# Loading, centring and multiplying the first two row tiles in another order

## The chip, the cores and the metric

The kernel runs on one core of a Trainium2 chip. The core has five engines that run side by side: TensorE (PE in the profile; its weight loads are PEld), VectorE (DVE), ScalarE (ACT), GpSimdE (POOL) and SyncE (SP). They wait for each other through semaphores. SyncE and ScalarE each issue loads and stores on a queue of their own. The metric is the device time of one execution in microseconds (us), and of several runs the median counts.

## The reference

Both halves of the model get the same normalised input. Only this matters here:

```
xn = (x - mean(x)) / sqrt(var(x) + 1e-5)          # x: 2048 x 512, bf16
q, k, v = xn @ wqkv                               # 32 heads of 16
phi(a) = [softmax(a @ w_phi), softmax(-a @ w_phi)]
o = phi(q) @ (phi(k)^T v) / (phi(q) @ sum(phi(k)) + 1e-6)
h = (xn @ w_gate) * (xn @ w_up)                   # 2048 x 1792
out = x + o @ wo + h @ w_down
```

## The kernel before, in words

The 2048 rows of x are 16 tiles of 128 rows. TensorE contracts over the partitions, so that every product with xn needs xn transposed: `xnT`, four blocks q of 128 columns for each tile. Tiles 4 to 15 are normalised on VectorE and transposed by DMA. Tiles 0 to 3, with which the kernel starts, take a shorter way: they are only centred, transposed on TensorE, and their scale (`rstd`) is applied later, on what is computed from them.

The way of a first tile t:

- `load_x_half` (L276) or `load_x` (L271) brings it in; a half is 256 of the 512 columns. A load that is issued earlier on a queue is begun earlier there.
- `ln_mean_split(t)` (L435) takes the mean in two parts at once: ScalarE sums the second half of the columns (an ACTIVATE and a read of its accumulator, L228), VectorE the first half (L438). For tiles 0 and 1 VectorE's part waits for the first half alone.
- `ln_center_split(t)` (L442) subtracts both parts in two instructions of 256 columns on VectorE (L445); `ln_center_whole(t)` (L449) does it in one of 512.
- `x_transpose(t, b, h, eng)` (L477) transposes half h, that is two blocks, on TensorE (L485) into PSUM bank b; then ScalarE (L228), or VectorE if it is named (L494), copies the result into `xnT`.
- `v_matmul(t, b, qs)` (L540) multiplies the blocks of `xnT` by the blocks of the v weights (`load_v`, L313), four matmuls of 512 columns for a tile, accumulated in bank b. All matmuls of this kind have line 247, in the helper `mm`.

Each call of `load_x_half`, `load_x` or `load_v` is one load on its queue. Before the change the queues begin so, in order: SyncE tile 0's first half, tile 1's first half, tile 2, v blocks 0 and 2, tile 3, then the gate and up weights (`load_gu`); ScalarE tile 0's second half, tile 1's second half, v blocks 1 and 3.

`warm` (L1008) issues matmuls on constants whose result nobody reads, into bank 7. The kernel begins with seven of 512 columns, and an eighth that waits for tile 0.

A small scheduler stands behind all this. Each helper records steps with what they read and write; `_order` (L1262) then plans the order on every engine by estimated costs. Steps recorded while `sc.pin` is set keep their recorded order on their engine. This is so for all of TensorE's steps, and from L329 to L350 and L1019 to L1056 for the steps of every engine. An instruction thus waits behind whatever is recorded ahead of it on the same engine, even if its own inputs are there. The order of the start is therefore the order of the lines L1017 to L1056: first the means and centrings of tiles 0 and 1, the transposes of both, then the v matmuls of both tiles together, block by block (q = 1 and q = 0 of both, tile 2's transposes, q = 3 and 2 of both). After them come tile 2's v matmuls and `g0a`, the first half of the first unit of the gate product (four matmuls of 256 columns), tile 3's transposes, and `u0a`, the same for the up product.

After the start, TensorE computes the gate and up products (L247) for all tiles with the attention's products in between, and at last the output products.

Of the kernel before, what the change touches and what calls it, by code (L numbers as in the profile page):

```python
# [10 lines left out]
ALU = mybir.AluOpType  # L11
AX = mybir.AxisListType

PE, ACT, DVE, POOL, SP = "PE", "ACT", "DVE", "POOL", "SP"
# [95 lines left out]
def bass_parallel_sum__linear_kernel_hedgehog__glu_gated_bilinear__prompt_kernel(  # L110
    nc: bass.Bass,
    A_x: bass.AP,
    A_wqkv: bass.AP,
    A_w_phi: bass.AP,
    A_wo: bass.AP,
    B_x: bass.AP,
    B_w_gate: bass.AP,
    B_w_up: bass.AP,
    B_w_down: bass.AP,
    out: bass.AP,  # L120
):
    with ExitStack() as es:
        _build(nc, es, A_x, A_wqkv, A_w_phi, A_wo, B_w_gate, B_w_up, B_w_down, out)


def _build(nc, es, A_x, A_wqkv, A_w_phi, A_wo, B_w_gate, B_w_up, B_w_down, out):
# [77 lines left out]
    def sb(name, lo, n):  # L204
        off = layout[name] + lo
        return arena[:, off:off + n]
# [4 lines left out]
    def sbf(name, lo, n):  # L211
        off = layout[name] + 2 * lo
        return arena[:, off:off + 2 * n].bitcast(F32)

    def bank(b, lo=0, n=512):
        return psum[:, b * 512 + lo:b * 512 + lo + n]

    def bank16(b, lo, n):
        return psum16[:, b * 1024 + lo:b * 1024 + lo + n]
# [3 lines left out]
    def act(out_ap, in_ap, reads, writes, func=ACTF.Copy, scale=1.0, bias=None, accum=None):  # L223
        kw = {} if bias is None else {"bias": bias}
        if accum is not None:
            kw["accum_out"] = accum
        n = out_ap.free_size()
        return sc.step(ACT, lambda e: e.activation(out=out_ap, in_=in_ap, func=func, scale=scale, **kw),  # L228
                       reads, writes, 130.0 + 0.833 * n)

    def dve(fn, reads, writes, n, rate=1.04):
        return sc.step(DVE, fn, reads, writes, 140.0 + rate * n)
# [7 lines left out]
    def mm(out_ap, pairs, reads, b, start=True, stop=True, skip=False, also=()):  # L240
        npair = len(pairs)

        def fn(e):
            ins = None
            for i, (l, r) in enumerate(pairs):
                kw = {"skip_group_check": True} if skip else {}
                ins = e.matmul(out_ap, lhsT=l, rhs=r, start=start and i == 0, stop=stop and i == npair - 1, **kw)  # L247
            return ins
        return sc.step(PE, fn, reads, [("ps", b), *also], npair * pe_cost(out_ap.free_size()))
# [8 lines left out]
    def x_tile(t):  # L258
        return sb("x", t * 512, 512)

    def xnT(q, lo, n):
        return sb("xnT", q * S_TOK + lo, n)


    def rows(ap, t0, n):
        g, r = divmod(t0, 4)
        if g == 0:
            return ap[t0 * 128:(t0 + n) * 128, :].rearrange("(r p) d -> p r d", r=n)
        return ap[g * 512:(g + 1) * 512, :].rearrange("(p r) d -> p r d", r=4)[:, r:r + n, :]

    def load_x(t0, n, eng=SP):  # L271
        o = sb("x", t0 * 512, n * 512).rearrange("p (t d) -> p t d", t=n)
        i = rows(x_flat, t0, n)
        sc.dma(eng, lambda e: e.dma_start(o, i), [], [("x", t) for t in range(t0, t0 + n)], n * 131072)

    def load_x_half(t, h, eng):  # L276
        c = slice(h * 256, h * 256 + 256)
        o, i = x_tile(t)[:, c], rows(x_flat, t, 1)[:, 0, c]
        sc.dma(eng, lambda e: e.dma_start(o, i), [], [("x", t) if h else ("x", t, 0)], 65536)  # L279
# [18 lines left out]
    def load_w(eng, o, i, key, nbytes):  # L298
        sc.dma(eng, lambda e: e.dma_start(o, i), [], [key], nbytes)
# [13 lines left out]
    def load_v(eng, q):  # L313
        load_w(eng, wv_v[:, q, :], A_wqkv[q * 128:(q + 1) * 128, 1024:1536], ("wv", q), 131072)
# [12 lines left out]
    pool(c_fn, [], ["const"], 300)  # L327

    sc.pin = True  # L329
    for t in range(2):  # L330
        load_x_half(t, 0, SP)
        load_x_half(t, 1, ACT)
    load_x(2, 1)
    load_v(ACT, 1)
    load_v(SP, 0)
    load_v(ACT, 3)
# [68 lines left out]
    def xn_tile(t):  # L405
        return sb("xn", (t % 4) * 512, 512)

    mu = sbf("mu", 0, ND)
# [24 lines left out]
    mua = sbf("mua", 0, ND)  # L433

    def ln_mean_split(t):  # L435
        act(xn_tile(t)[:, 256:], x_tile(t)[:, 256:], [("x", t)], [("mu", t)], scale=1.0 / 512.0,
            accum=mu[:, t:t + 1])
        dve(lambda e: e.tensor_scalar(out=xn_tile(t)[:, :256], in0=x_tile(t)[:, :256], scalar1=1.0 / 512.0,  # L438
                                      scalar2=0.0, op0=ALU.mult, op1=ALU.add, accum_out=mua[:, t:t + 1]),
            [("x", t, 0) if t < 2 else ("x", t)], [("mua", t)], 256)  # L440

    def ln_center_split(t):  # L442
        for h in range(2):
            hs = slice(h * 256, (h + 1) * 256)
            dve(lambda e, hs=hs: e.tensor_scalar(out=xn_tile(t)[:, hs], in0=x_tile(t)[:, hs], scalar1=mua[:, t:t + 1],  # L445
                                                 scalar2=mu[:, t:t + 1], op0=ALU.subtract, op1=ALU.subtract),
                [("x", t), ("mua", t), ("mu", t)], [("xn", t, h)], 256, 0.27)

    def ln_center_whole(t):  # L449
        dve(lambda e: e.tensor_scalar(out=xn_tile(t), in0=x_tile(t), scalar1=mua[:, t:t + 1],  # L450
                                      scalar2=mu[:, t:t + 1], op0=ALU.subtract, op1=ALU.subtract),
            [("x", t), ("mua", t), ("mu", t)], [("xn", t, 0)], 512, 0.27)
# [24 lines left out]
    def x_transpose(t, b, h, eng=ACT):  # L477
        n = NQ // 2
        qs = slice(h * n, (h + 1) * n)

        def fn(e):
            ins = None
            for i in range(n):
                q = h * n + i
                ins = e.transpose(bank16(b, i * 128, 128), xn_tile(t)[:, q * 128:(q + 1) * 128], ident)  # L485
            return ins
        sc.step(PE, fn, [("xn", t, h if t < 2 else 0), "ident"], [("ps", b)], n * 60.0)
        o = sb("xnT", 0, NQ * S_TOK).rearrange("p (q s) -> p q s", q=NQ)[:, qs, t * 128:(t + 1) * 128]
        i = bank16(b, 0, n * 128).rearrange("p (q s) -> p q s", q=n)
        w = [("xnT", t, h)]  # L490
        if eng == ACT:
            act(o, i, [("ps", b)], w)
        else:
            dve(lambda e: e.tensor_copy(out=o, in_=i), [("ps", b)], w, n * 128)  # L494
# [45 lines left out]
    def v_matmul(t, b, qs=((0, 1), (2, 3)), start=True, stop=True):  # L540
        for n, part in enumerate(qs):
            mm(bank(b), [(xnT(q, t * 128, 128), wv_v[:, q, :]) for q in part],
               ([("xnT", t, part[0] // 2)] if t < ND else [("xnT", t)]) + [("wv", q) for q in part], b,
               start=start and n == 0, stop=stop and n == len(qs) - 1)
# [463 lines left out]
    def warm(n, w=512, after=()):  # L1008
        def fn(e):
            ins = None  # L1010
            for _ in range(n):
                ins = e.matmul(bank(7, 0, w), lhsT=nc.const_aps.tensor(1.0, (128, 128), BF16),
                               rhs=nc.const_aps.tensor(1.0, (128, w), BF16), start=True, stop=True)
            return ins
        sc.step(PE, fn, after, [("ps", 7)], n * w * 0.8)

    warm(7)  # L1017
    warm(1, 512, [("x", 0)])
    sc.pin = True  # L1019
    ln_mean_split(0)  # L1020
    ln_mean_split(1)
    ln_center_split(0)
    ln_center_split(1)
    x_transpose(0, 2, 0)
    ln_mean_split(2)
    x_transpose(0, 3, 1)
    warm(1, 128)
    x_transpose(1, 4, 0, DVE)
    ln_center_whole(2)
    x_transpose(1, 5, 1, DVE)  # L1030
    warm(1, 128)
    for q in (1, 0):
        for t in range(2):
            v_matmul(t, t, ((q,),), start=q == 1, stop=False)
    x_transpose(2, 6, 0)
    x_transpose(2, 4, 1, DVE)
    for t in range(2):
        v_matmul(t, t, ((3,), (2,)), start=False)
    ln_mean_split(3)
    ln_center_whole(3)  # L1040
    (g0a, u0a, g0b, u0b), gate0 = up_unit(*ups.pop(0), pairs, 2)
# [366 lines left out]
```

The softmax here doesn't subtract the row's maximum and nothing guards it: scores larger than these inputs give would overflow.

## Time and profile before

| | us |
|---|---|
| median of 5 runs (lowest, highest) | 214.39 (214.08, 214.93) |
| the profiled execution | 214.34 |
| its span, first to last instruction | 212.6 |
| TensorE busy | 209.0 (98% of the span) |
| VectorE / ScalarE / GpSimdE busy | 165.9 / 144.8 / 108.7 |
| first instruction of TensorE (a warm-up) | 0.82 |
| first v matmul | 5.81 |
| end of the first gate half unit, `g0a` | 9.61 |

The profile covers one execution. The page has the busy time of each engine, the span in 40 slices, the chain of work that ended last, the costliest groups of instructions and the loads. The timeline lists an engine's instructions by start; the chain cut to a window lists what the end waited for, by start, length and what; the view of stretches gives busy times and counts of each engine between two moments. In a line such as `L247 PE MATMUL ps<-arena 128x512`, L247 is the line of the kernel (often a helper's), `ps` is PSUM and `arena` the one SBUF tensor that holds everything. A "q" behind an engine's name (SPq, ACTq) means its queue's issue of a load. The matmuls of TensorE are pipelined: the time shown for one reaches over the start of the next, and so the distance from start to start is what one costs.

### The profile page before, as it was taken

How to read it: one execution, taken by the hardware profiler on the slowest of the kernel's cores; microseconds unless marked ns; L12 is line 12 of the kernel's file. 1: busy time of each engine (PE TensorE's matmuls, PEld its weight loads, DVE VectorE, ACT ScalarE, POOL GpSimd, SP SyncE). 2: the span in 40 equal slices, each digit the busy share in tenths (PEclk: the TensorE clock that was granted, in tenths of full speed). 3: DMA queues.
4: the chain of work that ended last, by engine and by line, in shares of the span. 5: the costliest groups of instructions: out<-in, count | busy, mean ns of one | idle time of the engine just before them, and what ended most of it. 6: DMA issues, size and time to landing. Idle time of an engine off the chain costs nothing.

```text
span 212.6 us, 4050 instructions
## 1 busy us (share of the span) xinstructions
PE 209.0 (98%) x1476; PEld 125.6 (59%) x1476; DVE 165.9 (78%) x281; ACT 144.8 (68%) x350; POOL 108.7 (51%) x137
## 2 busy tenths in 40 slices
PE   8999999999999999999999999999999999999995
PEld 3565444444454444444444444556888898899884
DVE  3588699998986647758889989896888898897622
ACT  5459998885989999987878977564544444432220
POOL 4030393243312448998895472204658549558540
DMA  5999218479400320231321223413255826745411
GB/s 170 284 262 369 107 34 192 83 207 336 90 3 0 49 49 3 57 61 35 72 52 28 49 52 49 102 55 68 45 81 130 192 50 154 173 80 149 123 49 49
DMA packets 49795, 22.29 MB, mean 105 GB/s; under 512 B 38128, under 2 KB 48496, under 8 KB 49776
## 3 DMA queue, kind: packets, MB, share of 16 engines
q1 hardware_dynamic: 49200, 21.65, 42.3%
q10 hardware_dynamic: 576, 0.39, 0.6%
q8 instruction: 11, 0.18, 0.4%
q14 instruction: 8, 0.07, 0.1%
HBM read 11.03 MB, written 2.10 MB: 62 GB/s over the span
## 4 chain that ended last, share of the span: by engine, by line
PE 96%; DMA 2%; DVE 0%; ACTq 0%; ACT 0%; issue 0%
PE ps L247 91%; PE ps L564 2%; PE ps L622 2%; DMA arena<-in_A_wqkv_dram 2%; PE ps L392 1%; DVE arena L935 0%; ACTq L279 0%; PE ps L485 0%; ACT L1206 0%
## 5 line engine op out<-in xcount | busy, mean ns | idle before, releaser
L247 PE MATMUL ps<-arena 128*128 128x512 bf16 (+2 forms) x1160 | 200.1, 330 | 0.2 <-DMA arena<-in_A_wqkv_dram 0.2
L247 PEld LDWEIGHTS ps<-arena 128*128 128x128 bf16 (+1 forms) x1160 | 110.8, 98 | 74.0 <-issue 0.7
L228 ACT ACTIVATE arena<-ps 128x512 bf16<-128x512 f32 (+3 forms) x117 | 59.3, 538 | 17.8 <-PE ps L247 12.4
L228 ACT ACTIVATE arena<-arena 128x32 f32<-128x32 f32 (+8 forms) x131 | 52.4, 424 | 6.0 <-DVE arena L905 3.0
L905 DVE TENSOR_TENSOR arena<-ps,arena 128x512 f16<-128x512 f32 (+1 forms) x56 | 38.4, 686 | 19.6 <-ACT arena L228 13.7
L527 POOL TENSOR_TENSOR arena<-arena 128x1024 bf16<-128x1024 bf16 x16 | 30.9, 1933 | 38.1 <-ACT arena L228 38.1
L228 ACT ACTIVATE arena<-ps,arena 128x512 bf16<-128x512 f32 (+1 forms) x55 | 35.5, 671 | 10.1 <-PE ps L247 10.0
L517 DVE TENSOR_REDUCE arena<-arena 128x64 f32<-128x1024 bf16 x32 | 38.6, 1211 | 3.4 <-ACT arena L228 3.4
L866 POOL TENSOR_TENSOR arena<-arena 128x256 f16<-128x256 f16 x32 | 24.2, 768 | 12.9 <-DMA arena<-arena 11.7
L228 ACT ACTIVATE ps<-ps 128x256 f32<-128x256 f32 x24 | 8.8, 368 | 29.0 <-PE ps L247 29.0
L844 DVE TENSOR_TENSOR arena<-arena 128x896 f16<-128x896 f16 x32 | 23.8, 750 | 3.2 <-PE ps L247 3.1
L935 DVE SCALAR_TENSOR_TENSOR arena<-ps,arena 128x256 bf16<-128x256 f32 (+1 forms) x24 | 13.5, 569 | 10.4 <-PE ps L247 10.0
L784 POOL TENSOR_TENSOR arena<-arena 128x512 f16<-128x512 bf16 x14 | 16.2, 1175 | 4.7 <-DVE arena L905 3.3
L970 POOL TENSOR_TENSOR arena<-arena 128x512 f32<-128x512 f32 x8 | 9.5, 1190 | 17.2 <-ACT arena L228 17.2
L533 POOL TENSOR_TENSOR arena<-arena 128x512 bf16<-128x512 bf16 x16 | 17.1, 1074 | 0.9
L632 DVE TENSOR_TENSOR arena<-ps,arena 128x512 f16<-128x512 f32 x16 | 11.0, 688 | 1.4
L416 DVE BATCH_NORM_STATS2 arena<-arena 128x6 f32<-128x512 bf16 x16 | 10.4, 670 | 0.0
L531 POOL TENSOR_TENSOR arena<-arena 128x32 f32<-128x32 f32 x16 | 4.2, 266 | 9.5 <-ACT arena L228 9.5
L679 DVE BATCH_NORM_STATS2 arena<-arena 128x6 f32<-128x512 bf16 x14 | 9.0, 681 | 0.0
L564 PEld LDWEIGHTS ps<-arena 128*128 128x128 bf16 x128 | 6.1, 97 | 3.5
L813 DVE TENSOR_TENSOR arena<-arena 128x1792 f16<-128x1792 f16 (+1 forms) x8 | 7.0, 903 | 0.0
L622 PEld LDWEIGHTS ps<-arena 128*128 128x128 bf16 x128 | 6.2, 97 | 1.2
(54 smaller groups left out, 68.1 us busy)
## 6 DMA issues: line engine op xcount, KB each, us to landing
arena<-in_A_x_dram SPq DMA_DIRECT2D x8, 256.0 KB, 3.0
out_dram<-arena SPq DMA_DIRECT2D x15, 128.0 KB, 2.0
arena<-in_B_w_down_dram SPq DMA_DIRECT2D x1, 1792.0 KB, 7.5
arena<-in_A_x_dram SPq DMA_DIRECT2D x3, 512.0 KB, 4.2
arena<-arena SPq DMA_TRANSPOSE x44, 3.1
arena<-in_B_w_gate_dram SPq DMA_DIRECT2D x1, 640.0 KB, 8.7
arena<-in_B_w_up_dram SPq DMA_DIRECT2D x1, 640.0 KB, 9.9
arena<-in_B_w_gate_dram SPq DMA_DIRECT2D x1, 512.0 KB, 5.3
```

The costliest lines, as they stand in the source:

```text
L228: return sc.step(ACT, lambda e: e.activation(out=out_ap, in_=in_ap, func=func, scale=scale, **kw), reads, writes, 130.0 + 0.833 * n)
L247: ins = e.matmul(out_ap, lhsT=l, rhs=r, start=start and i == 0, stop=stop and i == npair - 1, **kw)
L517: dve(lambda e: e.tensor_reduce(out=sm, in_=e_v, axis=AX.X, op=ALU.add), [(name, s, 0), (name, s, 1)], [("sums", sr)], 1024)
L527: pool(lambda e: e.tensor_tensor(out=e_w, in0=e_w, in1=r_w, op=ALU.mult), [(name, s, 0), (name, s, 1), ("rs", n)], [(name, s, 0), (name, s ...
L533: pool(lambda e: e.tensor_tensor(out=e_v[:, :, 1, :], in0=e_v[:, :, 1, :], in1=rat[:, :, None].to_broadcast([128, H, 16]), op=ALU.mult), [ ...
L622: ins = e.matmul(bank(b0 + c // 4, (c % 4) * CW, CW), lhsT=ph[:, c, :], rhs=kvz_v[:, c, :], start=True, stop=True)
L632: dve(lambda e: e.tensor_tensor(out=o_tile(t).rearrange("p (b h f) -> p b h f", b=2, f=16), in0=nd[:, :, :, 0:16], in1=w_v[:, r].unsqueeze ...
L784: pool(lambda e, ft=ft: e.tensor_tensor(out=hH_v[:, ft, 0:512], in0=hT_v[:, ft, 0:512], in1=r2w, op=ALU.mult), [("hT", ft, 0), "r2w", ("x" ...
L844: dve(lambda e, k=k, i0=i0, i1=i1, op=op: e.tensor_tensor(out=s_block(p, k), in0=i0, in1=i1, op=op), ks + more, [s_key(p, k)] + over.get(k ...
L866: pool(lambda e, k=k, i0=i0, i1=i1, op=op: e.tensor_tensor(out=so_block(p, k), in0=i0, in1=i1, op=op), ks + [("so", p, m) for m in more], ...
L905: dve(lambda e: e.tensor_tensor(out=h_v[:, ft, sg * 512:(sg + 1) * 512], in0=bank(bu), in1=g, op=ALU.mult), [("ps", bu), ("g", s)] + ([("j ...
L935: dve(lambda e: e.scalar_tensor_tensor(out=o, in0=src, scalar=inv, in1=resid, op0=ALU.mult, op1=ALU.add), keys + [rkey, "inv"], [("ostg", ...
```

## The change

Only tile 0 is still loaded in halves. Tile 1 is loaded whole, by ScalarE's queue, in the slot where its second half was; SyncE's queue loses the other half, so that tile 2 and all that follows there move up by one issue. VectorE's part of tile 1's mean then waits for the whole tile.

`ln_center_split` becomes `ln_center_half`, one half for each call, and the recorded order changes: tile 0's first half is centred ahead of tile 1's mean, its second half after it. Tile 2 is centred before tile 0's second half is transposed. On TensorE tile 0's transposes come first; then tile 0's v matmuls run with tile 1's transposes between them, ahead of all of tile 1's v matmuls; tile 2's transposes stand behind the first v matmul of tile 1. The first copy of tile 1's transposed blocks goes to ScalarE in place of VectorE. The eighth 512-column warm-up and one of the two of 128 columns are gone. What is computed stays the same.

```diff
--- before.py
+++ after.py
@@ -327,10 +327,10 @@
     pool(c_fn, [], ["const"], 300)
 
     sc.pin = True
-    for t in range(2):
-        load_x_half(t, 0, SP)
-        load_x_half(t, 1, ACT)
+    load_x_half(0, 0, SP)
+    load_x_half(0, 1, ACT)
     load_x(2, 1)
+    load_x(1, 1, ACT)
     load_v(ACT, 1)
     load_v(SP, 0)
     load_v(ACT, 3)
@@ -437,14 +437,13 @@
             accum=mu[:, t:t + 1])
         dve(lambda e: e.tensor_scalar(out=xn_tile(t)[:, :256], in0=x_tile(t)[:, :256], scalar1=1.0 / 512.0,
                                       scalar2=0.0, op0=ALU.mult, op1=ALU.add, accum_out=mua[:, t:t + 1]),
-            [("x", t, 0) if t < 2 else ("x", t)], [("mua", t)], 256)
-
-    def ln_center_split(t):
-        for h in range(2):
-            hs = slice(h * 256, (h + 1) * 256)
-            dve(lambda e, hs=hs: e.tensor_scalar(out=xn_tile(t)[:, hs], in0=x_tile(t)[:, hs], scalar1=mua[:, t:t + 1],
-                                                 scalar2=mu[:, t:t + 1], op0=ALU.subtract, op1=ALU.subtract),
-                [("x", t), ("mua", t), ("mu", t)], [("xn", t, h)], 256, 0.27)
+            [("x", t, 0) if t == 0 else ("x", t)], [("mua", t)], 256)
+
+    def ln_center_half(t, h):
+        hs = slice(h * 256, (h + 1) * 256)
+        dve(lambda e: e.tensor_scalar(out=xn_tile(t)[:, hs], in0=x_tile(t)[:, hs], scalar1=mua[:, t:t + 1],
+                                      scalar2=mu[:, t:t + 1], op0=ALU.subtract, op1=ALU.subtract),
+            [("x", t), ("mua", t), ("mu", t)], [("xn", t, h)], 256, 0.27)
 
     def ln_center_whole(t):
         dve(lambda e: e.tensor_scalar(out=xn_tile(t), in0=x_tile(t), scalar1=mua[:, t:t + 1],
@@ -1015,27 +1014,27 @@
         sc.step(PE, fn, after, [("ps", 7)], n * w * 0.8)
 
     warm(7)
-    warm(1, 512, [("x", 0)])
     sc.pin = True
     ln_mean_split(0)
+    ln_center_half(0, 0)
     ln_mean_split(1)
-    ln_center_split(0)
-    ln_center_split(1)
+    ln_center_half(0, 1)
+    ln_center_half(1, 0)
+    ln_center_half(1, 1)
     x_transpose(0, 2, 0)
     ln_mean_split(2)
+    ln_center_whole(2)
     x_transpose(0, 3, 1)
     warm(1, 128)
-    x_transpose(1, 4, 0, DVE)
-    ln_center_whole(2)
+    v_matmul(0, 0, ((1,),), stop=False)
+    x_transpose(1, 4, 0)
+    v_matmul(0, 0, ((0,),), start=False, stop=False)
     x_transpose(1, 5, 1, DVE)
-    warm(1, 128)
-    for q in (1, 0):
-        for t in range(2):
-            v_matmul(t, t, ((q,),), start=q == 1, stop=False)
+    v_matmul(0, 0, ((3,), (2,)), start=False)
+    v_matmul(1, 1, ((1,),), stop=False)
     x_transpose(2, 6, 0)
     x_transpose(2, 4, 1, DVE)
-    for t in range(2):
-        v_matmul(t, t, ((3,), (2,)), start=False)
+    v_matmul(1, 1, ((0,), (3,), (2,)), start=False)
     ln_mean_split(3)
     ln_center_whole(3)
     (g0a, u0a, g0b, u0b), gate0 = up_unit(*ups.pop(0), pairs, 2)
```

## Prediction

> **What bounds the kernel now.** I read the page first, the chain of waits that ended last second, cut to its first 12 us, then the timelines of VectorE (DVE) and the stretches of the start.
>
> ```profile
> PE 96%; DMA 2%; DVE 0%; ACTq 0%; ACT 0%; issue 0%
> ```
>
> ```profile
> 1.71 3.96 DMA arena<-in_A_wqkv_dram
> 5.67 0.14 issue
> 5.81 1.42 PE ps L247 x4
> 7.22 0.22 PE ps L485 x4
> 7.45 2.16 PE ps L247 x12
> 9.61 0.22 PE ps L485 x4
> ```
>
> The columns of the chain are start, length, what. TensorE (PE) sets the end, and from 5.81 on it hands over from group to group without a hole; the records of the single matmuls show no start-to-start distance that is longer than the work from 6.64 us to the end. So whatever TensorE loses or gains before about 6.6 us arrives whole at the end, and the change lives in just that stretch. What the chain waits for ahead of 5.81 is the load of block 1 of the v weights, issued by ScalarE (ACT) as its third load at 1.71 and landed at 5.67.
>
> The second limit is TensorE's own pace. Here are the stretches (length, then the busy time and the number of instructions of each engine):
>
> ```profile
> 0.82:3.76 2.94, 2.94 (x8) 1.01 (x8) 0.64 (x3) 1.97 (x5) 2.23 (x13) 1.00 0.54 142
> ...
> 5.81:6.61 0.80, 0.80 (x2) 0.22 (x3) 0.80 (x5) 0.48 (x3) 0.00 (x0) 1.00 0.89 262
> 6.61:9.01 2.40, 2.40 (x15) 1.22 (x14) 1.17 (x5) 0.78 (x3) 0.00 (x0) 1.00 0.95 277
> ```
>
> The eighth warm-up starts at 3.76, so seven start-to-start steps take 2.94 us, 0.42 each. The first two v matmuls, of the same 128x512 shape, still take 0.40 each (0.80 for x2). The chain's 2.16 us for x12 is eight of 512 columns and four of 256: 0.216 and 0.109 each. The pace doubles at about 6.64 us, 5.82 us after the first warm-up, although the profile prints a granted clock of 1.00 throughout. Two matmuls behind the gate run slow: 2 x (0.40 - 0.216) = 0.37 us of the end.
>
> The third thing to see is how loads land. The lines give queue, count, size and the median time from issue to landing:
>
> ```profile
> arena<-in_A_x_dram SPq DMA_DIRECT2D x2, 128.0 KB, 3.8
> arena<-in_A_wqkv_dram ACTq DMA_DIRECT2D x2, 128.0 KB, 4.0
> ...
> arena<-in_A_x_dram SPq DMA_DIRECT2D x2, 64.0 KB, 2.1
> arena<-in_A_x_dram ACTq DMA_DIRECT2D x2, 64.0 KB, 2.3
> ```
>
> By issue plus landing: tile 0 is whole at 2.9, tile 1 at 3.7 (256 KB in all), tile 2 at 5.5 and v block 1 at 5.67 (512 KB), blocks 0 and 3 at 6.0 and 6.2 (768 KB). The two queues' loads come in side by side, in pairs.
>
> **The change, step by step.** All against the profiled execution, 214.34 us with a span of 212.6; the median of the runs shown is 214.39, 0.05 above, so a difference carries over. I compare the end of the first half unit (the x12 group, g0a), at 9.61.
>
> (1) Loads. SyncE (SP) drops one half load, so its later issues come one slot, 0.46 us, sooner; ACT's slots stay. Tile 1 is now a whole 128 KB beside tile 2 in the second slot. It can't be earlier than the halves were (3.7) and, if it takes as long as the other 128 KB loads (3.8 to 4.0 from 1.23), not later than 5.2. By bytes it completes at 384 KB, midway between 256 KB (3.7) and 512 KB (5.67): 4.7; SP's earlier slot takes a little off. I take 4.6. V block 1 now comes beside block 0, at 640 KB, midway between 5.67 and 6.2: 5.95, less up to 0.46 for the earlier slot; I take 5.8 (5.5 to 6.0), and with the 0.14 from landing to start a gate of 5.95.
>
> (2) Tile 0's first half. DVE's order puts its centring ahead of tile 1's mean.
>
> ```profile
> 2.75 0.42 DVE L438 TENSOR_SCALAR_CACHE_REDUCE arena<-arena 128x256 bf16<-128x256 bf16 x1 [2.75 <-DMA arena<-in_A_x_dram]
> 3.09 0.08 DVE L438 DVE_READ_ACCUMULATOR arena<-arena 128x1 f32 x1
> 3.55 0.42 DVE L438 TENSOR_SCALAR_CACHE_REDUCE arena<-arena 128x256 bf16<-128x256 bf16 x1 [0.38 <-DMA arena<-in_A_x_dram]
> 3.90 0.08 DVE L438 DVE_READ_ACCUMULATOR arena<-arena 128x1 f32 x1
> 3.90 1.11 DVE L445 TENSOR_SCALAR arena<-arena 128x256 bf16<-128x256 bf16 x4
> ```
>
> The centring can start when ACT's half of the mean is out (3.24 + 0.19 = 3.43), at 3.5, and takes 1.11 / 4 = 0.28. Its two transposes start near 3.95 in place of 4.30. That gain of 0.35 is hidden, because the gate is at 5.95.
>
> (3) Tile 0's second half. It now stands behind tile 1's mean on DVE, a new wait: everything queued there (both centrings of tile 1, tile 2's mean) waits with it. From 4.6: mean 0.42, centring 0.28, then transposes at about 5.4. On ACT tile 1's mean (0.42 and 0.19) stands ahead of the copy of tile 0's first half (0.38): 4.6 + 0.6 + 0.4 = 5.6. Both are ready before 5.95, so the wait costs nothing; cover 0.35 us. If tile 1 lands at 5.2, the copy ends near 6.2 and the gate is 6.25.
>
> (4) Tile 1's four transposes move behind the gate. Before, all of them ran by 5.3, in the time TensorE waited for weights anyway. Now two follow the first v matmul and two the second. Four more at 0.056 (0.22 for x4 in the chain): +0.22. Their copies (0.28 to 0.38) are hidden: tile 1's first v matmul comes four 512-column matmuls later. The copy given to ACT meets an engine idle for 1.08 us at 6.3.
>
> (5) One 512-column and one 128-column warm-up go. Neither stands behind the gate before, so nothing is saved by itself. The removed filler did keep TensorE busy from 3.76 to 4.18.
>
> (6) Later stretches. The loads of gate and up weights land at 7.84 and 9.1 and are needed at 9.0 and 9.67, both later now. VectorE, ScalarE and GpSimdE get another order behind the start, as it is planned anew; TensorE's is fixed by hand. With no idle time on TensorE after 6.6 I put this at 0, within 0.2 either way.
>
> Sum with the pace doubling at 6.64 as before: from gate to end of g0a at full pace 12 x 0.216 + 4 x 0.109 + 8 x 0.056 + 0.17 (what the chain adds for the last one to drain: 1.42 less 1.25 between starts) = 3.65; the slow stretch adds half of 6.64 - 5.95, 0.35. So 5.95 + 3.65 + 0.35 = 9.95 against 9.61: **+0.34**, thus 214.39 + 0.34 = 214.7. It is +0.25 with a gate at 5.8 and +0.45 at 6.25 with 0.2 slow: the slow pace hides half of every shift of the gate.
>
> **The unknown price: when the pace doubles.** TensorE was never idle for over 0.53 us between starts before 5.81. Now it has nothing from about 4.2 to 5.4, and again from 5.7 to 5.95. The trace of before has no such hole, so I bound its cost. From below: no effect, 0. (A gain needs an earlier doubling with less work ahead of it, for which no row speaks.) From above: the 5.82 us from the first matmul to the doubling are counted anew from 5.95, so it comes at 11.77, and (11.77 - 6.64) / 2 = 2.6 us are lost. The forecast takes 0, as the whole stretch before it (warm-up from 0.82 to 3.8) stays; the rival takes half of the upper end, 1.3.
>
> [...]
>
> **Rivals.**
> - *The pace doubles late* (the other side: slower). Place: the hole between tile 0's first transposes and the first v matmul. Price 1.3 on top of 0.34: 216.0. It decides once the doubling is later than 7.2 us, since (7.2 - 6.64) / 2 + 0.34 is 0.64. For it: the hole is about 1.2 us where 0.5 was the longest, and 5.82 us at an almost unbroken stream were needed. Against it: the stream up to 3.8 is the same, and the runs of before spread over only 0.85 us.
> - *Tile 1 lands late* and becomes the gate through DVE's and ACT's order: gate 6.25, +0.45, 214.85. For it: all other 128 KB loads took 3.8 or more. Against it: less is queued ahead of it.
> - *Tile 0 really starts early* (what the new order makes possible): v block 1 lands by 5.1, the gate is tile 0's copy at 5.2 and the pace has doubled by then. 5.2 + 3.65 = 8.85, -0.76: 213.6. Both halves are needed; with an unchanged doubling it is 5.2 + 3.65 + 0.72 = 9.57, no change. Against it: the weights' landing at 5.67 is the chain's own row, and its bytes now have more beside them.
>
> **Chances.** Forecast 0.42, late tile 1 0.10, late doubling 0.40, early start 0.08. About 0.3% (0.64 us) is what a measurement of this kernel can tell from no change, that is 213.75 to 215.03. Forecast and late tile 1 end inside it: same 0.52. Late doubling ends beyond: slower 0.40. Early start: faster 0.08. The forecast's own range is 214.2 to 215.0; the range must reach most of the late doubling, so 213.9 to 216.3, leaving out the early start and the upper part of the late doubling.
>
> **What would show it.** Step 1: tile 1's landing near 4.6, block 1's near 5.8. Steps 2 and 3: transposes of tile 0 near 3.95 and 5.4. Step 4: matmul, two transposes, matmul, two transposes from 5.95. Pace: v matmuls 0.216 apart from 6.6 on, or still 0.42 at 8. After g0a, no holes. I am wrong if g0a ends before 9.4 (the gate moved earlier than I think), or after 10.3 (the doubling moved).

## The result, and the profile after

The changed kernel takes 214.66 us (median of 36 runs, 213.87 to 216.24) against 214.13 (median of 71, 213.43 to 215.78). The ratio is 1.0038, 95% interval 1.0025 to 1.005: slower by a little. One median does not describe it, though. The 36 times fall in two groups with nothing between 214.71 and 215.28:

```
                       lower group              upper group (above 215.2 us)
before   71 runs       70, median 214.12        1   (215.78)
changed  36 runs       20, median 214.29        16  (215.28 to 216.24, median 215.97)
```

The median of 214.66 is only where the lower group ends. The profiled execution took 214.65, span 212.9, and belongs to the lower group. Its chain, cut to the first 12 us (start, length, what):

```profile
2.21 4.60 DMA arena<-in_A_wqkv_dram
6.80 0.14 issue
6.94 0.81 PE ps L247 x3
7.74 0.22 PE ps L484 x4
7.97 1.95 PE ps L247 x11
9.91 0.22 PE ps L484 x4
```

The load that the chain waits for is no longer v block 1 but block 3, issued at 2.21 and landed at 6.80. The first gate half unit, `g0a`, ends at 9.91 in place of 9.61; the span grew by the same 0.3. The timeline of TensorE shows what happened ahead of it (lines are one lower than before):

```profile
4.13 0.39 PE L484 MATMUL ps<-arena 128*128 128x128 bf16 x2 [0.16 <-DVE arena L444]
4.73 0.39 PE L484 MATMUL ps<-arena 128*128 128x128 bf16 x2 [0.20 <-DVE arena L444]
4.91 0.31 PE L1011 MATMUL ps<-const-bfloat16-1.0 128*128 128x128 bf16 x1
5.02 0.58 PE L247 MATMUL ps<-arena 128*128 128x512 bf16 x1
5.44 0.28 PE L484 MATMUL ps<-arena 128*128 128x128 bf16 x2
5.55 0.38 PE L247 MATMUL ps<-arena 128*128 128x512 bf16 x1
5.77 0.28 PE L484 MATMUL ps<-arena 128*128 128x128 bf16 x2
6.94 0.81 PE L247 MATMUL ps<-arena 128*128 128x512 bf16 x3 [0.89 <-DMA arena<-in_A_wqkv_dram]
```

The first v matmul starts at 5.02, 0.79 us earlier than before, and from 5.44 the starts are 0.11 us (two transposes) and 0.216 us apart: the pace has doubled by then. Tile 0 does start early. But from 5.88 to 6.94 TensorE has nothing to do, since the matmul with block 3 is next in its order, and that hole takes more than the early start had gained.

That the start decides everything can be read over several profiles of this study. Take the start of the first up half unit, the next group of 256 columns behind tile 3's transposes (the rows below the second belong to runs that are described further down):

```
                                      first v   pace doubles   first up half unit   time     difference
before                                5.81      6.64 (starts)   9.67                214.34   204.67
changed                               5.02      5.42            9.97                214.65   204.68
changed, profiled again: 213.78       5.25      4.85            9.09                213.78   204.69
changed, profiled again: 214.38       5.20      by 4.1 (starts) 9.72                214.38   204.66
changed, profiled again: 215.82       5.23      9.76           11.15                215.82   204.67
changed, four warm-ups for seven      5.69     11.32           12.13                216.80   204.67
changed order and warm-up, old loads  5.54      9.36           11.09                215.76   204.67
```

The last column is the same within 0.03 us: in these profiles nothing behind the start differs in a way that costs. "Pace doubles" is the moment from which the trace's records have the clock as full; where a trace has no such record it is read from the distance of the matmuls. In the traces kept the records begin with that moment, so the mean clock of an execution is printed as 1.00 although the pace was half before it.

### The profile page after: what moved, and what is told of

Read it like the earlier page. It is cut to its first block, busy times and chain, and to the rows that moved or that the text cites. A ratio compares the mean times of both kernels' runs of the same rounds, so it can differ in the third digit from the quotient of the medians.

```text
span 212.9 us, 4045 instructions
## 1 busy us (share of the span) xinstructions
PE 208.2 (98%) x1474; PEld 125.0 (59%) x1474; DVE 165.7 (78%) x280; ACT 145.0 (68%) x351; POOL 108.4 (51%) x137
## 4 chain that ended last, share of the span: by engine, by line
PE 96%; DMA 2%; ACTq 0%; DVE 0%; ACT 0%; issue 0%
PE ps L247 91%; DMA arena<-in_A_wqkv_dram 2%; PE ps L563 2%; PE ps L621 2%; PE ps L392 1%; DVE arena L934 0%; ACTq L299 0%; ACTq L274 0%; PE ps L484 0%; ACT L1205 0%
```

## The experiments

**The upper group: is it the pace, or a load?** Two theories. By the clock theory an execution of the upper group is one in which TensorE was idle too much ahead of the gate (the moment at which the first v matmul can start), so that its pace doubles some microseconds later. By the landing theory some load comes 1.5 us later in it. First the eighth warm-up is put back:

```diff
     warm(7)
+    warm(1, 512, [("x", 0)])
     sc.pin = True
```

> The changed kernel with the eighth 512-column warm-up (the one that waits for tile 0) put back; nothing else. The changed kernel's runs fall in two groups, 20 of 36 between 213.9 and 214.7 us and 16 between 215.3 and 216.2. Clock theory: the upper group is executions in which the doubling of TensorE's pace comes a whole period later, because TensorE was idle too long ahead of the gate; filling 0.37 us of that idle time makes the upper group clearly smaller than 44% (below 25%), and the lower group stays at about 214.3. Landing theory: the upper group is executions in which a load (v block 3, or tile 1) lands 1.5 us later; the filler changes nothing of that, the share stays at 35 to 55%.

Measured: 10 runs between 213.86 and 214.91, 2 at 216.24 and 216.41. The upper group is down to 2 of 12, which fits the clock theory; but 2 of 12 against 16 of 36 can still be chance. The lower group's median is 214.31.

Then both other holes ahead of the v matmuls are filled, too:

```diff
+    warm(1, 512, [("x", 0)])
...
     x_transpose(0, 2, 0)
+    warm(4, 128)
     ln_mean_split(2)
...
+    warm(6, 128)
     v_matmul(0, 0, ((3,), (2,)), start=False)
```

> The changed kernel with the eighth warm-up back, and with four more 128-column warm-ups behind tile 0's first two transposes and six ahead of tile 0's v blocks 3 and 2, where the profile shows TensorE idle for 0.41 and 1.06 us. Clock theory: hardly an execution is in the upper group any more (under 10%), median 214.2 to 214.5, as the lower group of the changed kernel (214.3), as the fillers stand in idle time. Landing theory: 35 to 55% of the executions stay above 215.2.

Measured: 214.27, and all 11 runs between 213.97 and 214.57. The upper group is gone, and the lower is where it was: work on constants, which nobody reads, takes away the executions at 216. 0 of 11 against 16 of 36 is hardly chance.

The opposite, fewer warm-ups (`warm(4)` for `warm(7)`):

> The changed kernel with four 512-column warm-ups at the start in place of seven. Clock theory: hardly any window of TensorE is busy enough before the v matmuls, the pace doubles between 7.3 and 10.8 us in nearly every execution; no lower group is left, median 215.3 to 216.3, nothing below 214.6, and the profile shows v matmuls 0.42 us apart beyond 6.5 us. Landing theory of the upper group: the two groups of the changed kernel stay as they are, 40 to 60% of the executions between 213.9 and 214.8.

Measured: median 215.62, 214.69 to 216.80. Nothing is below 214.6, as expected, but the two groups are not there in the old places either: three of the 10 runs lie between 214.69 and 215.04. In the profile, at 216.80, the full clock comes at 11.32 us, later than the 7.3 to 10.8 of the expectation, which was the author's estimate. Both experiments move only matmuls on constants, and the times follow them in both directions. As the explanation of the group as a whole the landing theory falls with that.

What was missing was an execution of that group itself. The changed kernel was profiled three times more:

> The changed kernel once more, for one profile. If the execution is of the upper group (above 215.2 us), the clock theory expects full pace only from 8 us or later and no load that lands over 1 us later than in the first profile; the landing theory expects full pace before 7 us and one hole of 1 us or more on TensorE. If it is of the lower group it tells only how the landings vary.

> The changed kernel once more, a second look. In the upper group (above 215.2 us): full pace only from 8 us on by the clock theory; a hole of 1 us or more on TensorE at full pace by the landing theory. In the lower group it shows only how the landings vary.

> The changed kernel once more, a third look. In the upper group (above 215.2 us): full pace only from 8 us on by the clock theory; a hole of 1 us or more on TensorE at full pace by the landing theory. In the lower group it shows only how the landings vary.

Measured: 213.78, 214.38 and 215.82. The third is of the upper group. TensorE's timeline there:

```profile
4.16 0.40 PE L484 MATMUL ps<-arena 128*128 128x128 bf16 x2 [0.19 <-DVE arena L444]
4.94 0.39 PE L484 MATMUL ps<-arena 128*128 128x128 bf16 x2 [0.38 <-DVE arena L444]
5.12 0.31 PE L1011 MATMUL ps<-const-bfloat16-1.0 128*128 128x128 bf16 x1
5.23 0.63 PE L247 MATMUL ps<-arena 128*128 128x512 bf16 x1
5.66 0.42 PE L484 MATMUL ps<-arena 128*128 128x128 bf16 x2
5.87 0.63 PE L247 MATMUL ps<-arena 128*128 128x512 bf16 x1
6.30 0.42 PE L484 MATMUL ps<-arena 128*128 128x128 bf16 x2
6.51 1.48 PE L247 MATMUL ps<-arena 128*128 128x512 bf16 x3
7.79 0.63 PE L484 MATMUL ps<-arena 128*128 128x128 bf16 x4
8.22 2.87 PE L247 MATMUL ps<-arena 128*128 128x512 bf16 x11
```

There is no hole after 5.23 and no late load (block 3 at 6.29). But the three v matmuls take 1.48 us where the first profile shows 0.81, the four transposes 0.63 for 0.39, and so on up to the eleven. The clock record has the full pace from 9.76, and the starts agree: from 8.22 it takes 2.71 us to the next four transposes, where at 213.78 the same eleven take 1.94 (6.92 to 8.86), so that by the two paces 1.54 us of it were slow. Against the execution at 213.78, whose first v matmul starts at the same moment (5.25), the first up half unit starts 2.07 us later, and the time is 2.04 longer. So the cause is shown for this execution: it is the pace.

How the idle time brings the moment about is not shown. An estimate from the starts in the timelines, with 0.427 us for 512 columns (the three v matmuls from 6.51 to 7.79) and 0.21 for two transposes, gives the time for which TensorE had nothing to do ahead of the first v matmul:

```
                     idle from         and from         sum     pace doubles
before               4.19 to 4.30      5.39 to 5.81     0.53    6.64
changed              3.76 to 4.13      4.34 to 4.73     0.76    5.42
changed, 213.78      3.76 to 4.09      4.30 to 5.07     1.10    4.85
changed, 215.82      3.76 to 4.16      4.37 to 4.94     0.97    9.76
```

The execution with the longest idle time of the four has the full pace first, so in a single execution this sum does not decide it. The expectations speak of a period and of windows that are busy enough; that was the author's assumption, and the runs do not show either: 9.76 lies 4.91 us behind 4.85 and 4.34 behind 5.42, which gives no common step. What they show is how often it happens: 16 of 36 runs in the upper group, 2 of 12 with the eighth warm-up back, 0 of 11 with all holes filled. The kernel before was above 215.2 in 1 of 71 runs; with its runs beside the experiments it is 3 of 168. No trace of those three was kept, so whether they have the same cause is open.

Three of the executions above 216, 216.18 and 216.11 of the changed kernel and 216.53 with the loads alone, differ from all others on record in one thing: their mean granted clock is 0.992, and the others' 0.999 or more. The missing 0.008 of 214.4 us is 1.7 us by an estimate from these two numbers, nearly the 1.8 to 2.4 by which the three lie above the medians of their lower groups. When the clock was lower in them, and why, is not shown, as no trace of these three was kept.

**The parts by themselves.** The shorter warm-up in the kernel before (the line `warm(1, 512, [("x", 0)])` out):

> The kernel before without its eighth 512-column warm-up; loads and order as before. TensorE's idle time ahead of 5.81 us grows from 0.62 to about 1.04 us. Clock theory: an upper group above 215.2 us appears with the order and the loads of before, in 15 to 40% of the executions (before: 1 of 71), and the lower group stays at 214.1. Landing theory: no upper group, median 214.1 within 0.2.

Measured: 8 runs at 213.74 to 214.19, 3 at 215.45 to 216.03. The share fits the clock theory, but the profile, at 215.45, does not:

```profile
4.07 6.64 DMA arena<-in_B_w_up_dram
10.71 0.05 issue
10.75 3.33 PE ps L247 x25
```

This execution had its full clock at 6.02 and lost 1.6 us because one load (up weights of slice 0) landed at 10.71, 6.64 us behind its issue, where it took 5.0 in the profile of before: the last of its sixteen parts came 2 us after all the others (8.75). So a late load can make such a time, too. That the shorter warm-up alone makes an upper group is not shown.

The loads of the change in the kernel before (order and warm-ups as before):

```diff
-    for t in range(2):
-        load_x_half(t, 0, SP)
-        load_x_half(t, 1, ACT)
+    load_x_half(0, 0, SP)
+    load_x_half(0, 1, ACT)
     load_x(2, 1)
+    load_x(1, 1, ACT)
```

> The kernel before with the loads of the change alone: tile 1 whole on ScalarE's queue, tile 2 and all behind it one slot earlier on SyncE's; order and warm-ups as before. If the new loads cost by themselves (v block 3 landed at 6.8 in place of 6.2 in the changed kernel's profile), +0.1 to +0.5 us; all transposes of tile 1 and 0 then wait for tile 1 (landed at 3.9), about 0.2 us later, hidden unless v block 1 lands as early as 4.75, too. Clock theory: TensorE's idle time grows only a little, so under 15% of the executions are above 215.2. Landing theory of the upper group: 35 to 55% above 215.2, as the loads are those of the change.

Measured: 214.15, 10 of 11 runs between 214.06 and 214.32, one at 216.53. The new loads show no cost by themselves; the expected 0.1 to 0.5 did not come. Nor do they make the upper group: one run of 11 is above 215.2, where the landing theory had 35 to 55%.

The changed kernel with the loads of before, the same diff the other way round:

> The changed kernel with the loads of before (tile 1 in halves, tile 2 in the third slot): order and shorter warm-up alone. Clock theory: TensorE waits for v block 1 (5.67 us in the profile of before) with about 1.5 us of idle time ahead of it, so an upper group above 215.2 us stays, 25 to 60% of the executions, whatever the loads; the lower group is at 214.1 to 214.4. Landing theory of the upper group (the new loads make it): no upper group, median 214.1 to 214.3.

Measured: 6 of 12 runs between 213.89 and 214.75 (median 214.14), 6 between 215.25 and 215.96. The upper group comes with the order and the warm-up, whatever the loads. Its profile is of the upper group (215.76): v block 1 holds the gate until 5.54, and the full clock comes at 9.36.

**The hole ahead of block 3.** Tile 1's blocks 1 and 0 are put ahead of tile 0's blocks 3 and 2, with the eighth warm-up and the four fillers:

```diff
-    v_matmul(0, 0, ((3,), (2,)), start=False)
-    v_matmul(1, 1, ((1,),), stop=False)
+    v_matmul(1, 1, ((1,), (0,)), stop=False)
     x_transpose(2, 6, 0)
     x_transpose(2, 4, 1, DVE)
-    v_matmul(1, 1, ((0,), (3,), (2,)), start=False)
+    v_matmul(0, 0, ((3,), (2,)), start=False)
+    v_matmul(1, 1, ((3,), (2,)), start=False)
```

> The changed kernel with the eighth warm-up and the four 128-column fillers, and with the v blocks 1 and 0 of tile 1 and tile 2's transposes moved ahead of blocks 3 and 2 of tile 0, so that TensorE has work while v block 3 is on its way. If the wait for block 3 is what ate the earlier start (0.3 us filled with warm-ups in the run with all holes filled, 1.06 us in the changed kernel's profile), 0.2 to 0.6 us faster than the run with all holes filled (214.27): 213.7 to 214.1, and no upper group. If the next load (up weights of slice 0, landed at 9.1 to 9.9 us and needed at 9.67 in the profile of before) takes its place, no gain: 214.1 to 214.4, with a hole ahead of the first up half unit.

Measured: 214.08, all 12 runs between 213.69 and 214.32; against before 0.9997 (0.998 to 1.0013). That is 0.19 below the run with all holes filled, at the edge of what was expected (0.2 to 0.6, or 213.7 to 214.1), and no gain on the kernel before. Its chain shows why:

```profile
5.56 0.34 PE ps L247
5.89 0.12 PE ps L484 x2
6.02 0.02 issue
6.04 0.39 ACT arena L228
6.43 0.05 issue
6.48 0.60 PE ps L247 x2
```

Now the first matmul of tile 1 waits until ScalarE has copied tile 1's transposed blocks (6.04 to 6.43), a copy that the changed order hid behind three matmuls. The hole is still 0.31 us, and it ends at 6.48, when block 3 is there anyway (6.44).

Two more arrangements tried to have work in every hole, both with the eighth warm-up and the four fillers; the diffs show the main lines. One loads the v blocks ahead of tile 2, or beside it, multiplies by block 0 first (the reordered matmuls are not shown), and moves the first up half unit behind the second gate half unit:

```diff
-    load_x(2, 1)
+    load_v(SP, 0)
     load_x(1, 1, ACT)
+    load_v(SP, 2)
     load_v(ACT, 1)
-    load_v(SP, 0)
+    load_x(2, 1)
     load_v(ACT, 3)
-    load_v(SP, 2)
...
-    u0a()
     g1a()
     v_matmul(3, 3)
     v_keep(3, 3)
+    u0a()
     u1a()
```

> The changed kernel with all holes filled (eighth warm-up, four of 128 columns), the v blocks 0, 2, 1, 3 loaded ahead of tile 2 or beside it, tile 0 multiplied by block 0 first, blocks 3 last for both tiles, and the second gate half unit ahead of the first up half unit. If the start is bounded by the landing of the v blocks alone, the first half unit ends near 8.9 us in place of 9.7 (5.0 for the first v matmul, 3.65 of work, 0.2 slow), and the time is 213.3 to 213.8, no upper group. If the sum of all bytes bounds it (up weights of slice 0 land at 9.1 to 9.9 us whatever the order), the hole moves to the first up half unit and the time is 213.8 to 214.2.

Measured: 215.11 (214.49 to 217.14), worse. In its profile, at 214.84, the pace is full by 4.0, but tile 1 lands at 4.67 in place of 3.88, and tile 0's second half, which stands behind tile 1's mean on VectorE, comes late; TensorE waits for it for 0.98 us, and for tile 2's copy for 0.36 later. What makes the slowest of these runs is not shown.

The last one keeps the loads of the change and moves the first half of tile 1's transposes ahead of the first v matmul, tile 2's mean behind the copies, and `g0a` ahead of tile 2's v matmuls:

```diff
     x_transpose(0, 3, 1)
-    warm(1, 128)
-    v_matmul(0, 0, ((1,),), stop=False)
     x_transpose(1, 4, 0)
-    v_matmul(0, 0, ((0,),), start=False, stop=False)
+    v_matmul(0, 0, ((1,), (0,)), stop=False)
     x_transpose(1, 5, 1, DVE)
+    ln_mean_split(2)
+    ln_center_whole(2)
+    v_matmul(1, 1, ((1,), (0,)), stop=False)
     v_matmul(0, 0, ((3,), (2,)), start=False)
...
-    v_matmul(2, 2)
     g0a()
+    v_matmul(2, 2)
```

> The changed kernel with the loads of the change, the eighth warm-up and four of 128 columns, tile 1's first transposes ahead of the first v matmul, blocks 1 and 0 of both tiles ahead of blocks 3 and 2, tile 2's mean and transposes later, and the first gate half unit ahead of tile 2's v matmuls. Every hole that the profiles showed between 5 and 9 us has other work in it. The run with tile 1's blocks 1 and 0 ahead (median 214.08) still had 0.37 us of waiting ahead of tile 1's first v matmul; if nothing else binds, this one is 0.2 to 0.5 faster: 213.6 to 213.9, no upper group. If a load or a copy takes the place of that wait (v block 3 lands at 6.3 to 6.8, tile 2's copies come later), 214.0 to 214.3.

Measured: 214.30, all 12 runs between 213.95 and 214.87; ratio to before 1.0006 (0.9991 to 1.0021). The chain of its profile passes through a wait of the same kind, now for tile 2's centring:

```profile
6.74 0.42 DVE arena L449
7.16 0.05 issue
7.21 0.40 PE ps L484 x4
```

No version beat the kernel before. Three of the four with filled holes (35 runs, none above 215) show what the new order is worth without the pace in the way: 214.27, 214.08 and 214.30, between nothing and 0.2 us more than before. Where the expected gain of an early start goes can be read from one profile of each: it removes one wait and meets the next load or copy some tenths of a microsecond later.

## Why the prediction was right, and where it was not

The forecast was 214.7, the range 213.9 to 216.3; 214.66 came out, and the range holds both groups but for the lowest run (213.87). The agreement of the medians is largely chance. It put all executions near 214.7, and gave the two outcomes as alternatives of 0.42 and 0.40. Both happened, side by side, in the same program.

*Step 1, loads: wrong in size.* Tile 1 was expected at 4.6 and landed at 3.88, v block 1 at 5.8 and landed at 4.75. The three further profiles give 4.1 to 4.3 and 4.86 to 5.07. The step read the landing of one execution (5.67) as the place to which so many bytes bring it. But the same block with the loads of before landed at 4.85 and 5.40 in two other profiles: the 5.67 is the latest of three that are 0.8 apart, and not a fixed place. So the gate was 5.02 to 5.25, not 5.95.

*Step 2, tile 0's first half: right in kind.* The transposes start at 4.13 where 3.95 was worked out.

*Step 3, tile 0's second half: right in kind, wrong in price.* Its transposes start at 4.73 where 5.4 was worked out, as tile 1 is early. But the step put its wait for tile 1 at nothing, since the gate was thought to be the load of block 1. With that load at 4.75 to 5.07 the wait is no longer covered. The chain of the execution at 215.82 runs through it:

```profile
1.23 2.94 DMA arena<-in_A_x_dram
4.17 0.02 issue
4.19 0.43 DVE arena L438 x2
4.62 0.27 DVE arena L444
```

Tile 1 lands, VectorE takes its mean, then centres tile 0's second half, and the first v matmul stands behind that half's transposes. The chain at 213.78 runs the same way, from a landing at 4.30. So what bounds the start of tile 0 there is tile 1, through the new order on VectorE. That is the mechanism of the rival "tile 1 lands late", at an earlier time than it had.

*Step 4, tile 1's transposes behind the gate: as predicted,* two pairs between the matmuls, each 0.11 at full pace. Only the count of what hides their first copy was off: three matmuls stand between, not four, and they suffice.

*What no step named: block 3.* With the gate at 5.0 the next load is late; step 1 gave its landing no place in the sum and so put this wait at nothing. Block 3 lands at 5.9 to 6.8 in the four profiles of the changed kernel, and with the early start it is wanted at 5.9. The loss is 1.06 us in the first profile, 0.83 at 214.38 and 0.15 at 213.78. The sum of the prediction (5.95 + 3.65 + 0.35 = 9.95) became 5.02 + 3.65 + 0.20 + 1.06 = 9.93 against 9.91 measured: other terms, the same total, and that is luck. (Two side sums of the prediction are slightly off: with the gate at 6.25 its own terms give +0.49, not +0.45, and a doubling at 7.2 gives 0.62, not 0.64.)

*Step 5, the shorter warm-up, costed at nothing:* true in the lower group, and part of the reason for the upper one: with the eighth back 2 of 12 runs are left in it, with the other holes filled too none. The rival "the pace doubles late" had its place (the hole between tile 0's transposes and the first v matmul) and its direction right; its price was 1.6 over the kernel before, and the upper group's median lies 1.84 over it. It was wrong only in being an all-or-nothing case.

*The unknown price.* Its upper bound counted 5.82 us from the first matmul to the doubling. The runs show no such constant: from 0.82 on it took 4.60 us in the first profile, 4.03 at 213.78 and 8.94 at 215.82, with the same seven warm-ups. The last two are 2.04 us apart in time, inside the bound of 2.6. The reason for taking 0, that the whole stretch of warm-ups stays, did not hold: with it a price near 0 and one near 2 both came out.

*Rival "tile 0 really starts early", 0.08.* Its two conditions, block 1 by 5.1 and the pace by then, both held in the execution at 213.78. There `g0a` ends at 9.03, not 8.85: the gate is 0.05 later and the wait for block 3 takes 0.15. That is 0.58 earlier than in the profile before, of the 0.76 that the rival had. It is the fastest execution seen of this kernel, but only 0.35 below the median of the kernel before, whose profiled execution was itself 0.2 above that median.

*Step 6, the rest: right.* The 204.66 to 204.69 us between the start of the first up half unit and the end show that no order changed there in a way that costs.

## What to carry to other kernels

Where an engine is slow at first, as TensorE was here (0.427 us for 512 columns, later 0.216), try work in its idle time until the pace has doubled: here that took the runs above 215.2 from 16 of 36 to 0 of 11. A filler that looks free to remove because nothing waits for it may hold the pace of everything behind it. When a change shortens the way to the first real work, look for the next thing that this work needs, here the third weight block and a copy, before counting the gain. And where the times of one program fall in two groups, no median and no single profile describes it: profile until each group has been seen.

## What the runs showed of the hardware

TensorE took 0.427 us for 512 columns at first and 0.216 later. With the same seven warm-ups the pace doubled at 5.42, 4.85 and 9.76 us in three executions of the changed kernel, and the last two differ by 2.04 us in time. Matmuls on constants in TensorE's idle time ahead of that changed how often the late doubling's times came: 16 of 36 runs above 215.2 us without them, 2 of 12 with one of 512 columns, 0 of 11 with ten of 128 beside it. The same 128 KB load of v block 1 took 3.0 to 3.4 us from issue to landing in the four profiles of the changed kernel, and 3.1, 3.7 and 4.0 in three profiles with the loads of before. One load in these profiles (up weights, with the shorter warm-up in the kernel before) took 6.64 us from issue to landing, against 5.0 in the profile of before; it had the last of its sixteen parts land 2 us after the rest (10.71 against 8.75), and TensorE stood behind it for 1.6 us.
